# A planner that holds an operation back while the other engine has the SBUF port: linear attention and a Mish feed-forward on one core

## The chip, the cores and the metric

The kernel runs on one core of a Trainium2 chip. A core has five engines, each with its own queue that it works off in order: TensorE (PE, matrix products; its weight loads are PEld), VectorE (DVE), ScalarE (ACT), GpSimd (POOL) and SyncE (SP), which here only issues DMA transfers. Engines wait for one another through semaphores. The metric is the device time of one execution in microseconds, and smaller is better. The kernel before was run three times: 506.88 us in the median, 506.66 to 507.48.

## The reference

The inputs are x (2048 tokens of width 512), weights for attention with 32 heads of 16, and a feed-forward of width 1792; all is float32.

```python
xn = _layernorm(x, axis=-1)
s = _A_ref(xn, A_wqkv, A_w_phi, A_wo)
g = _silu(_B_ref(xn, B_w1, B_b1, B_w2))
return x + s * g

# _A_ref: linear attention
pq = jnp.einsum("bhsd,hdf->bhsf", q, w_phi)      # the same for pk
phi_q = jnp.concatenate([_softmax(pq, axis=-1), _softmax(-pq, axis=-1)], axis=-1)
kv = jnp.einsum("bhsf,bhsd->bhfd", phi_k, v)
z  = jnp.einsum("bhsf->bhf", phi_k)
num = jnp.einsum("bhqf,bhfd->bhqd", phi_q, kv)
den = jnp.einsum("bhqf,bhf->bhq", phi_q, z)[..., None] + 1e-6
o = num / den                                     # then @ wo

# _B_ref: dense, Mish, dense
h = jnp.einsum("bsd,df->bsf", x, w1) + b1
act = h * jnp.tanh(sp)                            # sp = softplus(h)
return jnp.einsum("bsf,fd->bsd", act, w2)
```

## The kernel before

The tokens lie in 16 tiles of 128. Every large product is made in float32r from a high and a low part of each operand (three products in place of one), so each operand is split: ScalarE copies the high part, and VectorE or GpSimd subtracts it to get the low one. The two dense layers use a seven-product scheme on quadrants of their operands (Winograd's form), which needs sums and differences of blocks besides.

The parts, by the letters that the order table uses, each with a number of a tile or block:

- `wq wk wv wo`: a weight is loaded, for q and k multiplied ("folded") with the feature map (tiles `wqf`, `wkf`), and split.
- `N`: load a tile of x, statistics, normalise (`x`), transpose on TensorE (`pt`), split (`xT`), store both forms in DRAM (`scr`, `raw`).
- `K`, `V`, `Q`: the projections of a tile, one product of 12 matmuls each (`k`, `v`, `q`). K and Q are followed by the double softmax: copy (`k0p`), maximum and minimum (`k0m`), two differences (`k0e`), exponential, sum (`k0s`), reciprocal (`k0r`), for K the scaling. `A` adds two key tiles into `kvp` (TensorE) and `zacc`.
- `z`: sums of keys, `zb`. `D`: the denominator of a query tile: `ez` = scores times `zb`, its sum `tz`, `den`, the scaling, and transposes into `ph`. Half of the heads lie in `ph1_0`, the other half in `ph1_1`.
- `Ua`, `Ub`: numerators of eight tiles for one half of the heads (`pn`), split into `oh`, `ol`. `O`: the output projection of a tile (`pw`), kept in DRAM as `so`.
- `L`, `P`, `M`, `R`: blocks of the normalised x, of w1 (first and again), and of w2. `Fa` to `Fd`: the four pieces of a unit of the first dense layer (`fx`, `fy`, `fz`), stored as `hd`.
- `G`: a unit of the second dense layer: load `r`, Mish, sums of blocks on `r` (128 or 256 columns each), split into `ah` and `al` (896 columns), 21 matmuls into `y`. Eight token pairs of seven units make 56, the last five of which are one unit. `E`: the final of a token pair: sums of `y` (`yc`, `yy`), Silu, times the attention output (`sr`), plus x (`xx`), store.

Who does what and when is decided at build time. Every operation is recorded first (class `Program`), each with the engines that may do it: `either` gives VectorE and GpSimd the choice, `copy` and `held` ScalarE and VectorE. The order on TensorE is the order of the parts in the table `ORDER`. For the others, `simulate` plays the program through with assumed costs: at each event it takes, for each engine that is free, the ready operation with the earliest due time (`late`), and `issue` then writes the program out by planned start times. So one instruction queue per engine results, and the chip has no further choice; all of it is issued from one line, L351 before and L360 after.

Two things in `simulate` concern the port. `locks` says which operations need the SBUF port that VectorE and GpSimd share: each of GpSimd's, and VectorE's with two tensor inputs, none of them in PSUM. In `go`, an operation with a lock that starts while the port is held until the time `port` is planned longer by what is left:

```python
if e in o.lock:
    dur += max(0, port - now)
    port = now + dur
```

And `PEN` is added to the due time of an operation on VectorE's list if GpSimd or ScalarE could do it too, so that VectorE takes it later.

Of the kernel before, what the change touches and what calls it, by code (L numbers as in the profile page):

```python
# [38 lines left out]
K7 K6 N12 P0 V6 N10 N11 L0 V8 K11 V9 Fa0 Fa3 K10 A3 A4 V11 V12 V10 Fb3 Fb0 Fc3 Fc0 K12 N14 Fd3 N13 P6 N15 Fd0 K14 A5  # L39
K15 V13 K13 P1 Fa1 Fa6 P4 V15 V14 Q3 Fb6 Fc6 Q2 Fb1 A7 A6 Fc1 Q0 Fd1 P5 z Q7 M2 Fa5 Fd6 D3 Fa4 Q4 Q1 Fb5 Fa2 Fc5 Fb2  # L40
Fb4 Q9 D2 Fc2 D7 Q12 Fd2 Fc4 Fd5 M4 Q5 D4 Q15 L1 Fa9 Fb9 Fd4 Fa11 Fb11 D1 Q6 Fc11 D6 M1 M6 Fc9 Fd11 Fd9 D0 Fa8 D12
Fa13 Fb13 Fc13 M0 Q10 Fb8 Fc8 Fd13 wo1 D9 D15 Fa7 D5 Fb7 Q8 Fd8 M3 Fc7 M5 Q11 Fd7 Fa10 Fa12 D8 D10 Fb12 Fb10 Fc10 Ua0
Fc12 Fd10 Fd12 Ub0 wo0 Q14 Q13 O6 D11 O1 D14 R4 O2 O7 O5 O3 D13 Ua1 O4 Ub1 O0 O11 O15 O12 O8 O13 R0 O9 R5 R1 R6 O14 G0
R2 G1 G2 R3 G3 O10 G4 G5 G6 G7 G8 G9 G10 G11 G12 G13 G14 G15 G16 G17 G18 G19 E0 G20 G21 G22 G23 G24 G25 E1 E2 G26 G27
G28 G29 G30 G31 G32 E3 G33 G34 G35 G36 G37 G38 G39 E4 G40 G41 G42 G43 G44 G45 G46 G47 E5 G48 E6 G49 G50 G51 E7
"""
ACT_SET = {AF.Exp: 1, AF.Silu: 3, AF.Mish: 2}

# [5 lines left out]
class Program:  # L54
# [125 lines left out]
    def simulate(self, at):  # L180
# [17 lines left out]
        pos, now = 0, 0  # L198
# [1 line left out]
        busy = dict(BEGIN)  # L200
        aset = 0
        half = False
        dma = port = 0
        code, fetched, cold = HEAD, 0, 0
        lanes = []
        events = [(t, 2, -1) for t in BEGIN.values()]
# [6 lines left out]
        def fits(o):  # L213
            for t in {self.tag[n] for n in o.new}:
                mine = [n for n in o.new if self.tag[n] == t]
                if t == "ps" and "PE" in o.impl:
                    if free[t] < len(mine):
                        return False
                    continue
                before = 0  # L220
                for n in want[t]:
                    if n in mine:
                        break
                    before += 1
                if free[t] < before + len(mine):
                    return False
            return True
# [59 lines left out]
        while left:  # L287
            if not events:
                bad = [o for o in ops if o.start is None][:5]
                raise RuntimeError(f"no progress at {now}: {[(list(o.impl), o.writes, o.late, o.ready, o.new) for o in bad]} {free}")  # L290
            now, kind, i = heapq.heappop(events)
            todo = [(kind, i)]
            while events and events[0][0] <= now:
                _, kind, i = heapq.heappop(events)
                todo.append((kind, i))
            for kind, i in todo:
                if kind == 0:
                    o = ops[i]
                    o.ready = now
                    if "PE" not in o.impl:  # L300
                        for e in o.impl:
                            heapq.heappush(ready[e], (o.late + (PEN if e == "V" and len(o.impl) > 1 else 0), o.idx))
                elif kind == 1:
                    o = ops[i]
                    left -= 1
                    for n in o.reads | o.writes:
                        if n in uses:
                            uses[n] -= 1
                            if uses[n] == 0:
                                free[self.tag[n]] += 1  # L310
# [674 lines left out]
```

## Time and profile before

| | us |
|---|---|
| median of three runs (lowest, highest) | 506.88 (506.66, 507.48) |
| span of the profiled execution | 505.5 |
| TensorE busy | 496.5 |
| VectorE busy | 434.1 |
| ScalarE busy | 279.4 |
| GpSimd busy | 378.1 |

The span runs from the first to the last instruction. The median of the runs lies 1.4 us above it, for what lies around the span. The granted TensorE clock was 0.999 of full speed, so no throttling has to be told apart here. "Busy" counts an operation from its start to its end, with the time in which it waits for the port; a full engine is therefore not an engine at work all the time. Durations of neighbours on VectorE overlap by some tens of nanoseconds.

### The profile page before, as it was taken

The numbers are of one execution on the slowest core, as the hardware profiler recorded it, in microseconds if no ns is written. First come the engines' busy times: TensorE is split into PE (matmuls) and PEld (weight loads), VectorE is DVE, ScalarE is ACT, GpSimd is POOL, SyncE is SP. The second block draws the span as 40 slices with busy tenths as digits, with TensorE's granted clock in tenths as the row PEclk, the third lists the DMA queues.
The fourth block names the chain that finished last, engine by engine and source line by source line (L and its number), as shares of the span: only waits on it lengthen the run. The fifth ranks groups of instructions, "written<-read, shape, count | busy, mean of one in ns | idle before, by whom it ended". The sixth has DMA issues, their size and how long they took to land.

```text
span 505.5 us, 9803 instructions
## 1 busy us (share of the span) xinstructions
PE 496.5 (98%) x3594; PEld 426.6 (84%) x3594; DVE 434.1 (86%) x651; ACT 279.4 (55%) x412; POOL 378.1 (75%) x271
## 2 busy tenths in 40 slices
PE   8999999999999999999999999899999999999996
PEld 7888888888887888888888777678899999999996
DVE  5999999978879787999997899998768679978764
ACT  4865765465545332553233356587685775958611
POOL 2489999288786565686579558999789779789860
PEclk9999999999999999999999999999999999999999
DMA  8799898829987999889979762825463467665441
GB/s 307 227 336 302 294 346 278 269 105 316 294 295 251 332 319 326 291 233 318 337 240 345 255 229 78 294 89 188 146 209 118 147 204 241 236 199 171 147 146 63
DMA packets 96191, 120.35 MB, mean 238 GB/s; under 512 B 7568, under 2 KB 65040, under 8 KB 96144
## 3 DMA queue, kind: packets, MB, share of 16 engines
q1 hardware_dynamic: 96000, 119.70, 71.2%
q8 instruction: 28, 0.46, 0.4%
q14 instruction: 19, 0.16, 0.1%
q10 hardware_dynamic: 144, 0.03, 0.0%
HBM read 71.08 MB, written 48.63 MB: 237 GB/s over the span
## 4 chain that ended last, share of the span: by engine, by line
PE 89%; DVE 9%; ACT 1%; issue 0%; DMA 0%; DVEq 0%; ACTq 0%
PE y L351 28%; PE fx L351 15%; PE v L351 8%; PE fy L351 8%; PE q L351 8%; PE k L351 7%; PE pw L351 5%; PE fz L351 4%; PE pn L351 2%; PE kvp L351 2%; PE wake L351 1%; PE pt L351 1%; DVE ph L351 1%; DVE tz L351 1%; DVE ol L351 1%; DVE q13e L351 1%
## 5 line engine op out<-in xcount | busy, mean ns | idle before, releaser
L351 POOL TENSOR_TENSOR al<-r,ah 128x896 fp32r<-128x896 f32 (+1 forms) x26 | 55.0, 2123 | 11.2 <-ACT ah L351 9.7
L351 POOL TENSOR_TENSOR r<-r 128x128 f32<-128x128 f32 (+1 forms) x68 | 53.7, 808 | 4.8 <-DVE r L351 2.4
L351 ACT ACTIVATE ah<-r 128x896 fp32r<-128x896 f32 (+1 forms) x56 | 46.2, 853 | 16.5 <-POOL r L351 8.3
L351 DVE TENSOR_TENSOR al<-r,ah 128x896 fp32r<-128x896 f32 (+1 forms) x30 | 40.3, 1358 | 10.7 <-ACT ah L351 5.5
L351 ACT ACTIVATE r<-r 128x512 f32<-128x512 f32 x56 | 33.8, 624 | 19.4 <-DMA r<-hd 19.0
L351 DVE TENSOR_TENSOR r<-r 128x128 f32<-128x128 f32 (+1 forms) x52 | 38.8, 766 | 6.4 <-ACT r L351 3.5
L351 PE MATMUL k<-wkh,xT 128*128 128x512 f32 x128 | 42.2, 393 | 0.0
L351 PE MATMUL q<-wqh,xq 128*128 128x512 f32 x128 | 42.0, 393 | 0.0
L351 PE MATMUL y<-w2t,ah 128*128 128x256 f32 x224 | 40.9, 283 | 0.0
L351 PEld LDWEIGHTS y<-w2t,ah 128*128 128x128 f32 x224 | 34.9, 192 | 0.0
L351 PE MATMUL y<-w2t,al 128*128 128x256 f32 x112 | 31.7, 283 | 0.0
L351 PEld LDWEIGHTS q<-wqh,xq 128*128 128x128 f32 x128 | 24.0, 188 | 5.6 <-issue 0.7
L351 PEld LDWEIGHTS k<-wkh,xT 128*128 128x128 f32 x128 | 24.0, 188 | 5.0
L351 PE MATMUL y<-w2h,ah 128*128 128x256 f32 x96 | 27.2, 283 | 0.0
L351 PE MATMUL y<-w2l,ah 128*128 128x256 f32 x96 | 27.2, 283 | 0.0
L351 PE MATMUL y<-w2h,al 128*128 128x256 f32 x96 | 27.1, 283 | 0.0
L351 PE MATMUL k<-wkl,xT 128*128 128x512 f32 x64 | 24.9, 390 | 0.0
L351 PE MATMUL q<-wql,xq 128*128 128x512 f32 x64 | 24.9, 389 | 0.0
L351 PE MATMUL v<-wv0h,xT 128*128 128x512 f32 x64 | 23.1, 401 | 0.1
L351 PE MATMUL v<-wv1h,xT 128*128 128x512 f32 x64 | 22.3, 390 | 0.0
L351 PEld LDWEIGHTS y<-w2t,al 128*128 128x128 f32 x112 | 21.5, 192 | 0.0
L351 PE MATMUL y<-w2g,al 128*128 128x256 f32 x72 | 20.4, 283 | 0.0
(629 smaller groups left out, 1745.6 us busy)
## 6 DMA issues: line engine op xcount, KB each, us to landing
r<-hd SPq DMA_DIRECT2D x56, 256.0 KB, 3.8
scr<-xT SPq DMA_DIRECT2D x16, 512.0 KB, 5.3
xq<-scr SPq DMA_DIRECT2D x16, 512.0 KB, 5.6
w1b<-w1d SPq DMA_DIRECT2D x14, 512.0 KB, 5.7
w1b<-w1d SPq DMA_DIRECT2D x14, 384.0 KB, 4.7
x<-x SPq DMA_DIRECT2D x16, 256.0 KB, 4.7
raw<-xr SPq DMA_DIRECT2D x16, 256.0 KB, 4.6
fr<-raw SPq DMA_DIRECT2D x8, 512.0 KB, 6.4
```

Of the source, the lines that this page charges most:

```text
L351: getattr(e, m)(*a, **k)
```

## The change

`PEN` goes from 2000 to 0: an operation with a choice is no longer due later on VectorE. The new rule in `simulate`: an operation that locks the port is passed over while another holds it (`port > now + PTOL`, with `PTOL` 0), and the next ready one is tried; the time at which the port comes free is entered as an event, so that what was passed over is looked at again. The table `ORDER` holds the same parts in another order.

```diff
-PEN, HOLD, MARGIN = 2000, 300, 1000
+PEN, HOLD, MARGIN, PTOL = 0, 300, 1000, 0
...
-wq0 wk0 N4 N2 N1 N8 wk1 wv1 wv0 N0 K1 V0 K0 K4 N5 K2 wq1 V2 N3 K5 V3 V1 K3 N9 A0 V4 V5 K8 b1 P2 N7 N6 K9 A1 A2 P3 V7
...
-Fc12 Fd10 Fd12 Ub0 wo0 Q14 Q13 O6 D11 O1 D14 R4 O2 O7 O5 O3 D13 Ua1 O4 Ub1 O0 O11 O15 O12 O8 O13 R0 O9 R5 R1 R6 O14 G0
...
+wk0 wv0 N1 N15 wk1 wq0 K1 N0 K15 N2 K0 N4 wv1 N3 V0 V2 V3 V1 K3 N5 N7 A0 K2 V4 N10 K5 K7 N6 V5 A1 V7 N9 P2 N14 N11 K6
...
+Ua0 Fb10 R0 Fc10 Q13 O3 Q14 D11 Fd10 R1 O1 O4 D14 O7 O2 G7 D13 O5 R3 Ub1 R4 O6 G8 R2 Ua1 G0 O0 O9 O8 G9 G1 O12 O14 O11
...
+G25 G26 G27 G14 G32 G42 E3 G15 G33 G43 G34 G44 G45 G16 G46 G17 G47 G48 E4 G18 G49 E6 G19 G20 G50 E2 G51 E7
...
-                skip = []
+                skip, held = [], False
...
+                    if e in o.lock and port > now + PTOL:
+                        held = True
+                        skip.append((late, i))
+                        if len(skip) > 60:
+                            break
+                        continue
...
+                if held and port > told:
+                    told = port
+                    heapq.heappush(events, (port, 2, -1))
```

In the built program no kind of instruction is new. GpSimd's queue goes from 272 rows to 170, VectorE's from 637 to 744, ScalarE's from 415 to 407; TensorE and SyncE have as many as before.

TensorE at the start, before. `wqf` and `wkf` are folds, `pt` transposes of tiles of x, `k1` the first key product:

```order
L351 MATMUL wqf00_137<-phit_103,wqT00_134 128x128 x4
L351 MATMUL wqf01_138<-phit_103,wqT00_134 128x128 x4
L351 MATMUL wkf00_141<-phit_103,wkT00_130 128x128 x4
L351 MATMUL wkf01_142<-phit_103,wkT01_131 128x128 x4
L351 MATMUL pt4_149<-ident_83,x4_143 128x128 x4
L351 MATMUL pt2_157<-ident_83,x2_151 128x128 x4
L351 MATMUL pt1_165<-ident_83,x1_159 128x128 x4
L351 MATMUL pt8_173<-ident_83,x8_167 128x128 x4
L351 MATMUL wkf10_177<-phit_103,wkT10_132 128x128 x4
L351 MATMUL wkf11_178<-phit_103,wkT11_133 128x128 x4
L351 MATMUL pt0_191<-ident_83,x0_185 128x128 x4
L351 MATMUL k1_194<-wkh0_139,xT1_163 128x512
```

And of the change, the same place:

```order
L360 MATMUL wkf00_136<-phit_103,wkT00_130 128x128 x4
L360 MATMUL wkf01_137<-phit_103,wkT01_131 128x128 x4
L360 MATMUL pt1_147<-ident_83,x1_141 128x128 x4
L360 MATMUL pt15_155<-ident_83,x15_149 128x128 x4
L360 MATMUL wkf10_159<-phit_103,wkT10_132 128x128 x4
L360 MATMUL wkf11_160<-phit_103,wkT11_133 128x128 x4
L360 MATMUL wqf00_164<-phit_103,wqT00_161 128x128 x4
L360 MATMUL wqf01_165<-phit_103,wqT00_161 128x128 x4
L360 MATMUL k1_167<-wkh0_134,xT1_145 128x512
```

The first weight is that of the keys, and two transposes stand ahead of the first key product where five did.

VectorE ahead of the second pair of numerators, before: the last denominators (tiles 13 and 14) and the transposes into `ph1_0` and `ph1_1`, which the products `pn` read:

```order
L351 TENSOR_TENSOR q14r_838<-q14r_838,den14_860 128x64
L351 STREAM_TRANSPOSE ph1_0_724<-q11e_791 128x16x32
L351 TENSOR_TENSOR q13r_845<-q13r_845,den13_877 128x64
L351 STREAM_TRANSPOSE ph1_0_724<-q14e_842 128x16x32
L351 TENSOR_TENSOR q13e_849<-q13e_849,q13r_845 128x1024
L351 STREAM_TRANSPOSE ph1_0_724<-q13e_849 128x16x32
L351 STREAM_TRANSPOSE ph1_1_725<-q11e_791 128x16x32
L351 TENSOR_TENSOR w2e2_934<-w2r2_933 128x256
L351 STREAM_TRANSPOSE ph1_1_725<-q14e_842 128x16x32
L351 STREAM_TRANSPOSE ph1_1_725<-q13e_849 128x16x32
```

And of the change:

```order
L360 TENSOR_TENSOR q14r_849<-q14r_849,den14_868 128x64
L360 TENSOR_TENSOR q13r_840<-q13r_840,den13_880 128x64
L360 TENSOR_TENSOR w2e3_888<-w2r3_887,w2e3_888 128x256
L360 TENSOR_TENSOR q14e_853<-q14e_853,q14r_849 128x1024
L360 TENSOR_TENSOR q13e_844<-q13e_844,q13r_840 128x1024
L360 STREAM_TRANSPOSE ph1_1_619<-q14e_853 128x16x32
L360 STREAM_TRANSPOSE ph1_1_619<-q13e_844 128x16x32
L360 STREAM_TRANSPOSE ph1_0_618<-q14e_853 128x16x32
L360 STREAM_TRANSPOSE ph1_0_618<-q13e_844 128x16x32
L360 TENSOR_TENSOR w2e4_902<-w2r4_901 128x256
```

Both scalings (`q14e`, `q13e`) are on VectorE now, and `ph1_1` is ready first. On TensorE, the table puts `D11 Fd10 O1 O4 O7 O2 G7 O5` between the query product 14 and the numerators `Ub1`, where `O6 O1 O2 O7 O5 O3` stood between product 13 and `Ua1`.

VectorE at the end, before, from the last splits of the second dense layer to the last final (`yc1` and on):

```order
L351 TENSOR_TENSOR al7_5_1176<-r7_5_1174,ah7_5_1175 128x896
L351 TENSOR_TENSOR yc6_1149<-yy6_1150,y60_1129 128x256
L351 TENSOR_TENSOR yy6_1150<-yc6_1149,y61_1130 128x512
L351 TENSOR_TENSOR sr11_1143<-yy5_1141,sr11_1143 128x512
L351 TENSOR_TENSOR yy6_1150<-yy6_1150,y61_1130 128x256
L351 TENSOR_TENSOR xx11_1142<-sr11_1143,xx11_1142 128x512
L351 TENSOR_TENSOR yy6_1150<-yy6_1150,y62_1121 128x512
L351 TENSOR_TENSOR yy6_1150<-yy6_1150,y63_1122 128x512
L351 TENSOR_TENSOR sr13_1152<-yy6_1150,sr13_1152 128x512
L351 TENSOR_TENSOR xx13_1151<-sr13_1152,xx13_1151 128x512
L351 TENSOR_TENSOR yc1_1183<-yc0_1182,y70_1180 128x256
```

And of the change, the last twelve rows of the same stretch; ahead of them stand `al7_2` to `al7_4` and the sums and products of final 6:

```order
L360 TENSOR_TENSOR xx13_1146<-sr13_1147,xx13_1146 128x512
L360 TENSOR_TENSOR xx12_1148<-sr12_1149,xx12_1148 128x512
L360 TENSOR_TENSOR yc2_1159<-yy2_1160,y20_1114 128x256
L360 TENSOR_TENSOR yy2_1160<-yc2_1159,y21_1115 128x512
L360 TENSOR_TENSOR yy2_1160<-yy2_1160,y21_1115 128x256
L360 TENSOR_TENSOR yy2_1160<-yy2_1160,y22_1075 128x512
L360 TENSOR_TENSOR yy2_1160<-yy2_1160,y23_1076 128x512
L360 TENSOR_TENSOR sr5_1162<-yy2_1160,sr5_1162 128x512
L360 TENSOR_TENSOR sr4_1164<-yy2_1160,sr4_1164 128x512
L360 TENSOR_TENSOR xx5_1161<-sr5_1162,xx5_1161 128x512
L360 TENSOR_TENSOR xx4_1163<-sr4_1164,xx4_1163 128x512
L360 TENSOR_TENSOR yc1_1183<-yc0_1182,y70_1180 128x256
```

Before, VectorE did one of the two halves of finals 5 and 6 and GpSimd the other; now it does both halves of 6 and 2, one final behind the other.

More of the change, by code (lines that the diff above doesn't have):

```diff
@@ L37 @@
 ORDER = """
-wq0 wk0 N4 N2 N1 N8 wk1 wv1 wv0 N0 K1 V0 K0 K4 N5 K2 wq1 V2 N3 K5 V3 V1 K3 N9 A0 V4 V5 K8 b1 P2 N7 N6 K9 A1 A2 P3 V7
[L39 to L42, printed above, removed]
-Fc12 Fd10 Fd12 Ub0 wo0 Q14 Q13 O6 D11 O1 D14 R4 O2 O7 O5 O3 D13 Ua1 O4 Ub1 O0 O11 O15 O12 O8 O13 R0 O9 R5 R1 R6 O14 G0
-R2 G1 G2 R3 G3 O10 G4 G5 G6 G7 G8 G9 G10 G11 G12 G13 G14 G15 G16 G17 G18 G19 E0 G20 G21 G22 G23 G24 G25 E1 E2 G26 G27
-G28 G29 G30 G31 G32 E3 G33 G34 G35 G36 G37 G38 G39 E4 G40 G41 G42 G43 G44 G45 G46 G47 E5 G48 E6 G49 G50 G51 E7
+wk0 wv0 N1 N15 wk1 wq0 K1 N0 K15 N2 K0 N4 wv1 N3 V0 V2 V3 V1 K3 N5 N7 A0 K2 V4 N10 K5 K7 N6 V5 A1 V7 N9 P2 N14 N11 K6
+K4 K9 K10 N12 N8 V6 K11 K8 A2 P0 A3 V10 N13 V11 L0 V8 V9 P3 K12 A4 A5 b1 P4 V13 wq1 V14 V15 P6 K14 V12 K13 Fa3 Fa4 Fa0
+Fb0 Fc0 Fb3 Fd0 Fc3 Fb4 Q12 Fc4 Fa6 A7 A6 Fd3 Fb6 P1 Q4 M2 Q3 Fc6 Q7 Q2 P5 Fd6 z Fa5 D3 Fa1 D2 Fa2 Fb2 D7 Fb1 Fb5 Fc5
+Fc1 Fd5 Q1 Fc2 D12 Q6 Fd1 M4 L1 Fd2 Fa9 Fa11 Fd4 Q5 Fb9 Fb11 Fc11 D4 Fc9 Fd11 D1 Q11 M6 D6 M1 Q15 Q9 Q0 Fd9 M0 D0 D5
+Q8 Fa8 Fa13 Fb8 Fc8 Q10 Fb13 M5 Fa7 D9 Fd8 Fb7 Fc7 Fc13 Fd7 D15 D8 M3 D10 Ub0 Fa12 Fd13 Fb12 Fc12 Fa10 Fd12 wo1 wo0
+Ua0 Fb10 R0 Fc10 Q13 O3 Q14 D11 Fd10 R1 O1 O4 D14 O7 O2 G7 D13 O5 R3 Ub1 R4 O6 G8 R2 Ua1 G0 O0 O9 O8 G9 G1 O12 O14 O11
+O13 O10 G10 O15 R6 G11 G2 R5 G12 G13 E1 G35 G36 G3 G4 G5 G6 G37 G28 G38 G21 E0 G29 G22 G39 G40 G41 E5 G23 G30 G31 G24
+G25 G26 G27 G14 G32 G42 E3 G15 G33 G43 G34 G44 G45 G16 G46 G17 G47 G48 E4 G18 G49 E6 G19 G20 G50 E2 G51 E7
 """
@@ L202, in simulate @@
         half = False
-        dma = port = 0
+        dma = port = told = 0
         code, fetched, cold = HEAD, 0, 0
```

## The prediction, on record before the kernel ran

> **What bounds the kernel now.** I read the page's first part, then TensorE's waits, then the chain of waits, then the busy time by stage. The first rows are the span and the engines:
>
> ```profile
> span 505.5 us, 9803 instructions
> PE 496.5 (98%) x3594; PEld 426.6 (84%) x3594; DVE 434.1 (86%) x651; ACT 279.4 (55%) x412; POOL 378.1 (75%) x271
> ```
>
> TensorE is busy for 496.5 of 505.5 us, and the change neither adds nor drops a matmul. What can be won is therefore the 9.0 us in which TensorE stands idle; what can be lost has no such limit. The view of TensorE's own waits names four:
>
> ```profile
> PE pn L351 <- DVE ph L351: 1.4, 1, 1.4
> PE wake L351 <- DVE mhalf L452: 1.1, 1, 1.1
> PE pt L351 <- ACT x L351: 1.0, 1, 1.0
> PE pw L351 <- DVE ol L351: 0.8, 1, 0.8
> ```
>
> The wait before `wake` is the launch and stays. Most of the rest is the drain behind the last product. Three waits of 1.4, 1.0 and 0.8 us are open to a new order, 3.2 us together. Now the stages (columns: window, its length, then busy time of PE, PEld, DVE, ACT, POOL):
>
> ```profile
> 15.00:60.00 45.00, 44.90 (x277) 36.78 (x276) 44.49 (x82) 31.59 (x48) 37.83 (x29) 1.00 0.90 284
> 60.00:125.00 65.00, 65.00 (x596) 53.94 (x596) 59.52 (x86) 36.53 (x53) 50.92 (x33) 1.00 0.81 263
> 286.00:335.00 49.00, 46.82 (x666) 35.85 (x641) 47.30 (x86) 31.58 (x63) 40.38 (x25) 1.00 0.55 186
> 335.00:490.00 155.00, 155.00 (x1060) 144.68 (x1059) 125.50 (x140) 102.95 (x144) 132.72 (x110) 1.00 0.55 177
> ```
>
> VectorE is as full as TensorE between 15 and 60 us (44.49 of 45.00) and nearly so between 286 and 335 (47.30 of 49.00). Where both are full, a microsecond more on VectorE is a microsecond more for TensorE. The chain of waits says the same: it runs through VectorE in both places. Its row of a query product, twelve matmuls in 2.72 us, is the price of a product further down.
>
> ```profile
> 36.02 1.51 DVE k0e L351
> 37.53 0.61 DVE xT L351
> ...
> 141.91 2.72 PE q L351 x12
> ...
> 312.56 1.65 DVE ez L351
> ...
> 318.13 1.55 DVE q13r L351
> ...
> 320.34 1.60 DVE q13e L351
> ```
>
> Some of these pieces are not work. `q13r` is 64 columns wide and holds the chain for 1.55 us. Such time is waiting for GpSimd, as this pair shows:
>
> ```profile
> L351 DVE SCALAR_TENSOR_TENSOR den<-tz x16: 127/188/2332, 178.8 to 316.8; 128x32 f32<-128x32 f32 x16
> 265.78 2.39 POOL L351 TENSOR_TENSOR wo1l<-wor,wo1h 128x1024 fp32r<-128x1024 f32 x1 [0.74 <-DVE ha L351]
> 265.88 2.33 DVE L351 SCALAR_TENSOR_TENSOR den<-tz 128x32 f32<-128x32 f32 x1
> ```
>
> An operation whose median is 188 ns took 2.33 us, because a GpSimd operation of 2.39 us had begun 0.10 us earlier. The change tries to plan such pairs away.
>
> **What moves.** Counted in the built order, 102 tensor-tensor operations go from GpSimd to VectorE: 33 of 128 columns, 24 of 256, 23 of 512, 12 of 896, 10 of 1024. Twelve copies go from ScalarE to VectorE, and ScalarE gets four more table loads. The transfers are the same 354 rows on the SyncE queue in another order. Prices:
>
> ```profile
> L351 DVE TENSOR_TENSOR al<-r,ah 128x896 fp32r<-128x896 f32 x20 | 28.3, 1428 | 6.9 <-ACT ah L351 4.7 <-POOL al L351 2.0
> 470.10 1.08 DVE L351 TENSOR_TENSOR al<-r,ah 128x896 fp32r<-128x896 f32 x1
> L351 POOL TENSOR_TENSOR al<-r,ah 128x896 fp32r<-128x896 f32 x20 | 46.8, 2350 | 11.2 <-ACT ah L351 9.7 <-DVE al L351 1.3
> L351 DVE TENSOR_TENSOR r<-r 128x128 f32<-128x128 f32 x36 | 26.4, 746 | 1.1 <-POOL r L351 1.0
> L351 POOL TENSOR_TENSOR r<-r 128x128 f32<-128x128 f32 x44 | 30.0, 697 | 3.5 <-DVE r L351 2.4 <-PE y L351 0.6
> L351 POOL TENSOR_TENSOR r<-r 128x256 f32<-128x256 f32 x24 | 24.2, 1012 | 1.3 <-ACT r L351 1.3
> L351 DVE TENSOR_TENSOR xx<-sr,xx 128x512 f32<-128x512 f32 x6 | 9.3, 1558 | 1.3 <-POOL sr L351 1.2
> L351 POOL TENSOR_TENSOR xx<-sr,xx 128x512 f32<-128x512 f32 x8 | 12.4, 1555 | 2.3 <-DMA xx<-x 2.2
> L351 DVE TENSOR_TENSOR xT<-pt,xT 128x512 fp32r<-128x512 f32 x16 | 10.6, 675 | 1.7 <-ACT xT L351 1.7
> L351 DVE TENSOR_TENSOR u<-u,sr 128x256 f32<-128x256 f32 x4 | 1.7, 425 | 1.0 <-ACT u L351 1.0
> 245.49 1.22 DVE L351 TENSOR_TENSOR q0e<-q0e,q0r 128x1024 f32<-128x1024 f32 x1
> L351 DVE TENSOR_REDUCE tz<-ez 128x64 f32<-128x1024 f32 x16 | 19.0, 1199 | 0.0
> ```
>
> Undisturbed, VectorE takes 0.425 us for 256 columns, 0.675 for 512, 1.08 for 896, 1.22 for 1024, and by an estimate from the first two 0.30 for 128. The moved work is 33 x 0.30 + 24 x 0.425 + 23 x 0.675 + 12 x 1.08 + 10 x 1.22 + 12 x 0.675 = 69 us on VectorE. GpSimd loses, at its means, 33 x 0.70 + 24 x 1.01 + 23 x 1.56 + 12 x 2.35 + 10 x 2.4 = 135 us and falls to about 243.
>
> If every port wait stayed, VectorE would be busy for 434 + 69 = 503 us, longer than TensorE: then VectorE bounds the kernel. But waits are in the 434: 20 x (1.428 - 1.08) = 7.0 in `al`, 36 x (0.746 - 0.30) = 16.1 in the short `r`, and 6 x (1.558 - 0.675) = 5.3 in `xx`, so 28 in three groups alone. Without those VectorE is at 475. I take 480: the waits shrink at least with GpSimd's work, and a plan that holds operations back removes more, though not all. That is 46 us more than before, and the question is where.
>
> Mostly it is late. The units of the second dense layer (335 to 490) run almost wholly on VectorE now; there it was busy for 125.5 of 155 us and GpSimd for 132.7. About 80 of the 102 operations are of this stage (33 of 128 columns, 18 of 256, 16 of 512, 12 of 896), 9.9 + 7.7 + 10.8 + 13.0 = 41 us, which would make 166 with the old waits and about 138 without the 28. That fits under TensorE's 155, and I price it at 0, from 0 to +10.
>
> **Start: -0.8 us.** TensorE ran three folds and five transposes before the first `k`:
>
> ```profile
> 12.38 1.36 PE L351 MATMUL pt<-ident,x 128*128 128x128 f32 x8 [1.01 <-ACT x L351]
> 15.98 0.48 PE L351 MATMUL k<-wkh,xT 128*128 128x512 f32 x1
> 5.59 0.69 DVE L351 BATCH_NORM_STATS2 st<-x 128x6 f32<-128x512 f32 x1 [1.11 <-DMA x<-x]
> 6.56 1.95 PE L351 MATMUL wqf<-phit,wqT 128*128 128x128 f32 x16
> 7.23 1.07 POOL L351 TENSOR_TENSOR rs<-rs,mhalf 128x1 f32<-128x1 f32 x2 [5.30 <-DVE rs L351]
> 9.14 1.53 ACT L351 ACTIVATE x<-x,nb,rs 128x512 f32<-128x512 f32 x2 [0.88 <-DVE nb L351]
> ```
>
> Now there are three folds and two transposes. Before, 800 KB (scores' table, `wqT`, first `x`) were there at 5.59 us. In the new order the same 800 KB are both `x` tiles, the table and the first half of `wkT`, so the first fold can start when the warm-up ends, at 6.56, and takes 1.8 us (1.95 less the overlap), to 8.4. The second tile needs statistics (ends about 6.3), two small sums (0.3), both powers on GpSimd (1.07), a bias on VectorE behind the first tile's normalising (0.7) and one normalising on ScalarE (1.53 / 2): 9.2. Its transpose follows, then two folds of 1.8: `k` starts at about 13.4 where it started at 15.98. Three transposes are still owed, 1.36 / 2 = 0.6 each as the row has it. Gain 15.98 - 13.4 - 1.8 = 0.8. Bounds: -1.4 (the transposes hide their overhead) and +0.6 (`phit` now stands behind the first statistics).
>
> **Middle: -2.2 us.** Before, six attention products (2.72 us each, 16.3) stood between the last query product and the second pair of numerators, and VectorE's row of work in that time needed 1.4 more. Now two dense products, four attention products, a unit of the second layer and one more attention product stand there: 7 x 2.72 = 19.0 us. VectorE's rows from that query's score copy to the transposes that the numerator reads add up to 17.1 us by the prices above and the reductions' 1.2. So the 1.4 should go, if port waits there stay under 1.9. The 0.8 of `pw <- ol` goes as well: its attention product now comes 6.8 us behind the numerator instead of 5.4. Bounds: -2.2 and +2 (GpSimd has two products with `zb` in that chain).
>
> **Keys and values: +0.9 us.** All sixteen tiles' keys and values now come before the first dense product, where eleven keys and ten values came before. An estimate from the rows: TensorE needs 32 x 2.72 = 87 us for them, and with transposes, folds and key sums some 106; VectorE needs about 5.8 us a tile (statistics 0.69, split 0.675, maximum, minimum and differences at 0.675 each, the sum at 1.2, small ones), and with the weights' splits, the scaling and `zacc` some 107. VectorE has no slack of its own there, only what TensorE's lag behind it leaves. Some unplanned waits will show: from 0 to 5, and I take 0.9, nearer the old stage, for which the waits view names none.
>
> End: the drain behind the last product does not change, 0. Sum: -0.8 - 2.2 + 0.9 + 0 = -2.1. The profiled span 505.5 becomes 503.4; the median of the runs, 506.88, lies 1.4 above that span, so the forecast is 504.8 us.
>
> [...]
>
> **The rivals.** First: the waits only change place. VectorE has 46 us more to do, and each gain of 3.0 us is paid back in stalls of under a microsecond. For it: the full windows above. Against it: the two middle gaps are covered by more TensorE work now. Time 506.5, chance 0.18.
>
> Second, slower: VectorE bounds the key and value stage. Its place is the run of sixteen keys; its price two waits for a whole GpSimd operation (2.39 in the row), less a little that TensorE's queue hides, 4.5 in place of the 0.9. It decides once the stalls there pass the 3.0 us gained elsewhere. For it: 44.49 of 45.00. Time 506.9 - 3.0 + 4.5 = 508.4, chance 0.16.
>
> Third, slower: the end. All four multiplies and adds of a final are on VectorE, and two finals (tiles 6 and 2) stand between the last units' splits and the last final, where GpSimd took half of each:
>
> ```profile
> 489.75 1.62 POOL L351 TENSOR_TENSOR xx<-sr,xx 128x512 f32<-128x512 f32 x1
> 492.44 0.42 DVE L351 TENSOR_TENSOR yc<-yc,y 128x256 f32<-128x256 f32 x1 [2.22 <-ACT yc L351]
> 495.62 1.21 DVE L351 TENSOR_TENSOR yc<-yc,y 128x256 f32<-128x256 f32 x3 [2.76 <-PE y L351]
> ```
>
> A final is two operations of 256 and seven of 512 columns, 5.6 us, some 7 with its wait for Silu. Between the last two rows lie 26 matmuls, 0.12 us each; tile 2's last unit is done 24 + 52 = 76 matmuls, 9.1 us, ahead of the product that the last final needs. From 2 us of lag on, the end moves. With 6 us of lag: 504.8 + 4 = 508.8, chance 0.10.
>
> Fourth: everything opens, 1.4 at the start, 2.2 in the middle and nothing new: 506.9 - 3.6 = 503.3, chance 0.12.
>
> **How the numbers follow.** The forecast has 0.44, with a range of its own from 503.8 to 506.0. This kernel tells a change from none at about 0.2%, 1.0 us: faster is under 505.9, slower over 507.9. Faster is 0.42 of the forecast and the fourth, 0.54; the same is 0.02 of the forecast and 0.17 of the first, with 0.01 from the slower cases, 0.20; slower is the second and third with the rest, 0.26. The range from 503.0 to 508.7 leaves out a little of the fourth and the worse half of the slower ones.
>
> **What would show it.** Right: the `pn <- ph` and `pw <- ol` waits gone from TensorE's waits; `k` begins at about 13.4 us; VectorE busy near 480 and GpSimd near 245 us; `al` on VectorE near 1.1 us; no TensorE wait on a VectorE tile over 0.5 us before 125 us. Wrong: TensorE waiting for `xT`, `k..e` or a bank in the keys; GpSimd's fall without a fall of VectorE's means; the last `yc` waiting for VectorE and not for TensorE.

## The result and the profile after

The changed kernel takes 509.74 us in the median of four runs (508.2 to 510.4), the kernel before 506.77 us beside it (506.08 to 507.48). The ratio is 1.0052 with a 95% interval from 1.0033 to 1.007: slower by half a per cent, where 2.1 us less were forecast. A second set of six runs gave 509.06 against 507.18 us, ratio 1.0039 (1.0024 to 1.0055).

The page of the changed kernel, first part (span, then busy time, share and instructions of each engine):

```profile
span 506.5 us, 9767 instructions
PE 496.2 (98%) x3594; PEld 425.4 (84%) x3594; DVE 430.1 (85%) x765; ACT 278.8 (55%) x404; POOL 244.1 (48%) x169
```

TensorE's own waits there (us in total, times, longest):

```profile
PE pn L360 <- DVE ph L360: 2.7, 1, 2.7
PE wake L360 <- DVE mhalf L461: 1.1, 1, 1.1
PE fx L360 <- ACT hc L360: 0.7, 1, 0.7
PE fx L360 <- ACT hb L360: 0.4, 1, 0.4
PE wkf L360 <- DVE rs L360: 0.3, 1, 0.3
PE fx L360 <- DVE ha L360: 0.3, 1, 0.3
```

GpSimd lost a third of its work and VectorE, which took it over, is busy for 4 us less than before: most of its waiting for the port is gone. Yet the wait for `ph`, 1.4 us before, is 2.7 us now, and the dense products `fx` have three waits that the kernel before did not have. Of the old ones only `pw <- ol` and `pt <- x` are gone.

Where the time went is read from the busy time by stage. Two rows of the kernel before that the prediction does not show (window, length, then busy time of PE, PEld, DVE, ACT, POOL):

```profile
0.00:60.00 60.00, 57.72 (x362) 48.96 (x362) 53.50 (x109) 39.33 (x60) 41.64 (x43) 1.00 0.89 292
125.00:286.00 161.00, 161.00 (x841) 132.39 (x855) 141.78 (x219) 66.93 (x91) 111.04 (x64) 1.00 0.88 299
```

and the same view of the changed kernel:

```profile
0.00:60.00 60.00, 58.52 (x430) 49.96 (x431) 53.62 (x121) 41.41 (x64) 42.17 (x42) 1.00 0.92 299
60.00:125.00 65.00, 64.95 (x537) 53.57 (x536) 62.05 (x88) 34.35 (x48) 45.93 (x32) 1.00 0.81 263
125.00:286.00 161.00, 159.57 (x931) 129.60 (x930) 144.26 (x229) 66.18 (x92) 81.42 (x49) 1.00 0.84 287
286.00:335.00 49.00, 46.27 (x450) 36.66 (x464) 45.52 (x81) 30.58 (x52) 36.50 (x21) 1.00 0.58 195
335.00:490.00 155.00, 155.00 (x1171) 143.93 (x1140) 116.86 (x233) 104.23 (x145) 38.08 (x30) 1.00 0.57 184
```

TensorE's idle time, length less busy time, went from 2.28 to 1.48 us in the first 60 us, from 0 to 0.05 in the keys, from 0 to 1.43 between 125 and 286, from 2.18 to 2.73 between 286 and 335, and stayed at 0 in the second dense layer. That is -0.80 + 0.05 + 1.43 + 0.55 = +1.2 us; the profiled spans differ by 1.0. So the start brought what it should, and the loss lies in one stretch, from the query products to the last pair of numerators.

The medians differ by more than the profiled spans, because the executions of the changed kernel fall into two groups: of its second six, three spanned 506.2 to 506.7 us at a granted clock of 1.000, and three 508.0 to 508.5 at 0.996 to 0.997, while the kernel before lay between 504.2 and 506.0 at 0.998 to 1.000 throughout. The profile shown is one of the shorter kind, whose times (507.9 to 508.4 us) lie only some 1 us above the kernel before; the longer kind makes the rest of the difference, and is explained below by the last experiments' rows.

Now the stretch itself. The timeline of the changed kernel at 212 us (start, duration, operation), first VectorE's:

```profile
212.52 1.22 DVE L360 TENSOR_TENSOR t11l<-t,t11h 128x1024 fp32r<-128x1024 f32 x1
213.65 3.43 DVE L360 TENSOR_TENSOR t31l<-t,t31h 128x1024 fp32r<-128x1024 f32 x1
217.01 1.21 DVE L360 TENSOR_TENSOR t41l<-t,t41h 128x1024 fp32r<-128x1024 f32 x1
```

and GpSimd's:

```profile
212.74 3.26 POOL L360 TENSOR_TENSOR ez<-q4e,zb 128x1024 f32<-128x1024 f32 x1 [1.88 <-DVE t L360]
```

Three equal operations take 1.22, 3.43 and 1.21 us. The GpSimd product `ez` came in 0.2 us after the first had begun, waited for its end and then held the port; the second waited for it. The planner had meant it otherwise. These are the times with which it laid out the program (a model inside the kernel, not a measurement) beside the real ones:

```
operation                  planned start   real start (us)
t11l   VectorE                 211.67         212.52
t31l   VectorE                 212.80         213.65
t41l   VectorE                 213.94         217.01
ez (tile 4)   GpSimd           215.21         212.74
```

In the plan GpSimd is passed over until `t41l` ends. In the program nothing says so: the order within GpSimd's queue is kept, but `ez` waits only for what it reads and writes, and the row names the end of VectorE's `t` (212.6 us) as what released it. It starts 2.5 us ahead of its plan, and the wait that the rule planned away comes back, on the other engine. The planner of the kernel before lets an operation start at once and adds the wait for the port to its duration, as with `den` and `wo1l` in the prediction's rows. Up to 330 us VectorE lies at most 2.9 us behind that plan, and up to 7.9 us behind the new one.

The same view at 307 us, where 19 us later the late numerators begin, VectorE:

```profile
307.72 2.38 DVE L360 SCALAR_TENSOR_TENSOR den<-tz 128x32 f32<-128x32 f32 x1
```

and GpSimd:

```profile
307.64 2.41 POOL L360 TENSOR_TENSOR ez<-q13e,zb 128x1024 f32<-128x1024 f32 x1
```

Summed over the trace (each VectorE operation's duration above the fastest tenth of its operation and shape, where that is over 0.15 us), the waits fell from 29.2 to 18.0 us ahead of 327 us and from 54.8 to 2.6 behind. The big saving lies where TensorE was the bound in any case; ahead of 327 us, 11 us were saved against some 17 us of work that VectorE took over (the moved operations at undisturbed prices).

In both meetings the operation that came second took longer by about what the first still had to do: `ez` behind `t11l` by 0.87 us (3.26 in place of the 2.39 it takes alone, below), where `t11l` had 1.00 left, and `t31l` behind `ez` by 2.21 (3.43 against 1.22), where `ez` had 2.35 left. Not every operation of VectorE takes part. Of those of the changed kernel that began while a GpSimd operation had more than 0.6 us left, the 21 reductions of 1024 columns took 1.21 us in the median and the 45 operations on two tensors of 512 columns with one in PSUM 0.68, both as with GpSimd idle; the four on two tensors of 1024 columns in SBUF took 1.71 to 3.43 in place of 1.22. The same happened in the keys (2.2 us at 94 us, where TensorE lost 0.05 us in the whole stage), but what it cost came in the query stage.

### The profile page after: what moved, and what is told of

Same layout as the page of the kernel before. It is cut to its first block, busy times and chain, and to the rows that moved or that the text cites. A ratio compares the mean times of both kernels' runs of the same rounds, so it can differ in the third digit from the quotient of the medians.

```text
span 506.5 us, 9767 instructions
## 1 busy us (share of the span) xinstructions
PE 496.2 (98%) x3594; PEld 425.4 (84%) x3594; DVE 430.1 (85%) x765; ACT 278.8 (55%) x404; POOL 244.1 (48%) x169
## 4 chain that ended last, share of the span: by engine, by line
PE 42%; DVE 12%; issue 1%; DMA 1%; ACT 1%; POOL 0%; ACTq 0%; DVEq 0%
PE y L360 27%; PE pw L360 6%; PE fx L360 3%; PE pn L360 2%; DVE tz L360 2%; DVE ph L360 2%; PE fy L360 1%; PE q L360 1%; DMA w1b<-w1d 1%; DVE den L360 1%; PE fz L360 1%; DVE u L360 0%; DVE q6r L360 0%; DVE hc L360 0%; DVE ha L360 0%
## 5 line engine op out<-in xcount | busy, mean ns | idle before, releaser
L360 DVE TENSOR_TENSOR al<-r,ah 128x896 fp32r<-128x896 f32 (+1 forms) x43 | 42.6, 1011 | 9.5 <-ACT ah L360 8.0
L360 POOL TENSOR_TENSOR al<-r,ah 128x896 fp32r<-128x896 f32 (+1 forms) x13 | 24.9, 1927 | 47.4 <-ACT ah L360 32.9
L360 POOL TENSOR_TENSOR r<-r 128x128 f32<-128x128 f32 (+1 forms) x17 | 13.6, 812 | 49.4 <-DVE r L360 26.9
L360 DVE TENSOR_TENSOR r<-r 128x128 f32<-128x128 f32 (+1 forms) x103 | 30.6, 340 | 7.6 <-ACT r L360 6.9
L360 ACT ACT_TABLE_LOAD x15 | 19.2, 1283 | 7.8 <-DVE yy L360 6.4
```

Of the source, the lines that this page charges most:

```text
L360: getattr(e, m)(*a, **k)
```

## Which half of the change it is

The first four runs undo one half of the change each: the planner (`PEN` 2000 and the rule off), the order, and the planner in one stage alone.

```diff
e1, on the changed kernel
-PEN, HOLD, MARGIN, PTOL = 0, 300, 1000, 0
+PEN, HOLD, MARGIN, PTOL = 2000, 300, 1000, 10**9
e2, on the changed kernel
-ORDER = (the new table)
+ORDER = (the table of the kernel before)
```

> The new order of TensorE's parts with the old planner (penalty 2000 ns, rule off). Theory 1, VectorE bounds the query stage: in the changed kernel its own work up to the last transposes is 278 us at undisturbed prices against 260 before, while the waits that the rule saves there came to 12.5 us only. Here that work is 255 us, so VectorE is there earlier than in either kernel, TensorE's wait for ph (2.7 us in the changed kernel, 1.4 before) and its waits in the first dense layer (1.4 together) go, and the time is 504.5 to 505.5 us. Theory 2, the new order itself is at fault, because it puts the parts that wait too close together: TensorE's waits for hc, hb and ph stay, and the time is 509 to 510 us, as for the whole change.

> The old order of TensorE's parts with the new planner (penalty 0, rule on). VectorE's own work up to the last transposes is 267.5 us, 8 more than before. Theory 1 (VectorE's sum of work and port waits decides): plus 8 of work, minus some 12 of port waits, so VectorE is a little earlier than before, the wait for ph shrinks below 1.4 us and the time is 505 to 507 us. Theory 2 (the order is at fault): about 506.8 us, as before. Theory 3 (the planner's choice is bad with any order): 509 us or more, with new waits of TensorE for VectorE before 330 us.

```diff
e3, on the changed kernel (e4 has < in place of >=)
-(PEN if e == "V" and len(o.impl) > 1 else 0)
+((PEN if now >= 330000 else 2000) if e == "V" and len(o.impl) > 1 else 0)
-if e in o.lock and port > now + PTOL:
+if e in o.lock and port > now + PTOL and now >= 330000:
```

> The changed kernel, but penalty 0 and the rule hold only from the planner's 330 us on (second dense layer and end); up to there the old planner. Theory 1 (the loss is VectorE's extra work in the query stage): VectorE's own work up to the last transposes is 259 us as before, port waits there near 30 us again, and the time is 504.5 to 506 us. Theory 2 (order at fault): 509 to 510. Theory 4 (the loss is in the second dense layer or the end, where nearly all splits and finals are on VectorE): 509 to 510 as well, with VectorE's wait ahead of the last yc replaced by TensorE's work ending later; told from theory 2 by the first run.

> The changed kernel, but penalty 0 and the rule hold only up to the planner's 330 us; from there the old planner, with the second dense layer shared between VectorE and GpSimd as before. Theory 1: nothing changes up to the last transposes (278 us of work there), the waits for ph, hc and hb stay, and the time is 509 to 510 us as for the whole change; what the rule gained in the second dense layer was hidden under TensorE anyway. Theory 4 (loss in the second layer or the end): 506 to 507 us.

The first, the third and the fourth lie far from everything that was expected; the second fits theory 3 alone (509 us or more, with a new wait ahead of 330 us). Measured against 507.04 us of the kernel before: the order alone 558.41 us (ratio 1.1008, 1.0985 to 1.103), the planner alone 516.5 (1.0187, 1.0173 to 1.0201), the new planner only late 543.56 (1.0726, 1.0707 to 1.0746), only early 526.91 (1.0402, 1.038 to 1.0424). TensorE's longest waits with the order alone:

```profile
PE y L360 <- DVE yc L360: 8.5, 2, 7.7
PE fz L360 <- DVE hb L360: 6.4, 1, 6.4
PE kvp L360 <- POOL k8e L360: 4.4, 1, 4.4
```

with the planner alone:

```profile
PE pn L360 <- DVE ph L360: 5.3, 1, 5.3
```

and with the new planner early only:

```profile
PE y L360 <- DVE yc L360: 8.7, 2, 7.8
PE y L360 <- DVE yy L360: 3.5, 3, 2.5
```

A table of parts is good only with the planner that it was laid out for: each half alone costs 9 to 51 us, both together 2 to 3. So these runs cannot say which half of the pair costs the 3 us, and theories 1 and 2 are not decided by them. Theory 3, that the planner's choice is bad with any order, is left by the second run and falls with the next section, where the new planner with the new order beats the kernel before. The runs do say something of the second dense layer: with the old planner from 330 us on, TensorE waits there for `yc` and `yy`, 12 us together, and the kernel is 17 us slower than with the new one throughout (526.91 against 509.7). The relief there is needed by this table; it is not a gain over the kernel before.

The planner's own end of the last product foretold most of this, but not the change:

```
kernel                     planned end of products   measured span (us)   difference
before                            500.7                   505.5              4.8
order alone (e1)                  559.6                   556.4             -3.2
planner alone (e2)                510.1                   514.5              4.4
new planner late (e3)             531.6                   541.3              9.7
new planner early (e4)            515.6                   525.2              9.6
changed kernel                    493.8                   506.5             12.7
```

Behind the last product come some 4.8 us of drain. The last product of the kernel before ends where its plan says. The changed kernel was planned 6.9 us shorter and lies 8 us behind its plan: it is not that nothing was to be won, but that the chip did not follow. Part by part, TensorE's lag behind the plan grows from 1.3 us at 128 us to 2.2 at 222, 4.0 at 276, 7.1 at 326 and 7.9 at the end. This set the next theory.

## Making the hold real

Theory 5: the loss is the hold that stands only in the plan. The test keeps plan and order as they are and makes GpSimd wait in the program. Ahead of a GpSimd operation that the rule had passed over stands a GpSimd subtraction on one column, which reads a result of the VectorE operation that held the port (by `locks` that can also be a copy or a one-tensor operation outside PSUM).

```diff
+                        if e == "G":
+                            o.hold = owner
...
+            y = o.hold
+            if o.eng == "G" and y is not None and y.eng == "V":
+                t = (first column of y's result)
+                nc.gpsimd.tensor_tensor(self.pin, t, t, op=ALU.subtract)
             for m, a, k in o.impl[o.eng][1]:
```

> The changed kernel with the same plan and the same order on every engine; only ahead of each of the 45 GpSimd operations that the new rule passed over in the plan stands a GpSimd operation on one column that reads the result of the VectorE operation behind which the planner held it. So GpSimd really starts behind it. Theory 5 (the hold exists only in the plan: nothing in the program makes GpSimd wait, it starts as soon as its inputs are there, gets ahead of the VectorE operation and makes that one wait instead): VectorE's waits up to 327 us fall from about 15 us to under 5, TensorE's waits for ph, hc and hb go, and the time is 499 to 503 us. Theory 1 (VectorE's moved work is too much whatever GpSimd does): 508 to 511 us, as the changed kernel.

The second does it at four places only, `(o.part, y.part) in (("A4", "L0"), ("D4", "L1"), ("D5", "D6"), ("D13", "D11"))`:

> As the run before, but only at four places: zacc of key pair 4 behind t2 of the first load, the product of tile 4 with zb behind t4l, that of tile 5 behind the normalising of tile 6, that of tile 13 behind den of tile 11. There VectorE's t3, t3l, q6r and den11 waited 2.2, 2.2, 1.7 and 2.2 us, 8.3 together. Theory 5: most of the 8.3 us on VectorE go, the wait for ph goes, 503 to 506 us. Theory 1: 508 to 511 us.

The control has the same 45 operations, reading the constant `mhalf`:

> Control for the two runs before: the same 45 one-column operations on GpSimd, but they read a constant and wait for nothing. Theory 5 and theory 1 both: as the changed kernel, 508 to 511 us, since 45 short operations delay GpSimd by some 0.1 to 0.2 us each and it has half its time free. If it is under 506 us, the gain of the runs before was the delay alone and not the order.

> The changed kernel once more, for its spread and for a profile of one of its longer executions. All theories: median 508.5 to 510.5 us. Theory 5 asks that a longer execution differ from the shorter one by further VectorE operations of 0.1 to 0.7 us that wait for a whole GpSimd operation, with TensorE's wait for ph longer by as much; theory 6 (the granted clock alone makes the spread) asks for the same waits and longer matmuls.

All on one chip, beside 507.18 us of the kernel before: all 45 holds 504.64 us (ratio 0.9957, 0.9943 to 0.997), four holds 504.55 us (0.9951, 0.9938 to 0.9965), the control 508.63 (1.0028, 1.0017 to 1.0039), the changed kernel 509.06. Four small operations are worth 4.5 us, and they beat the kernel before by 0.5%; the same operations without the wait are worth 0.4 us, which is within the spread of both. Theory 5 stands, theory 1 in its strict form (VectorE's moved work is too much whatever GpSimd does) falls.

The control is not without any effect on the order: its profile (span 507.1 us) has `t31l` at 3.42 us and the `fx` waits of the changed kernel, but `den` at 0.30 us, because the added operations happened to delay `ez` past it, and so 1.1 us of waiting for `ph`. TensorE idles where it does not in the changed kernel (0.8 us between 60 and 125 us, 0.4 in the second dense layer); their cause was not looked for.

The size for 45 holds was missed: 499 to 503 us were expected, and VectorE's waits ahead of 327 us, by the sum above, fell to 9.9 us, not under 5 (four holds: 11.9; control 17.2). The 41 further holds clear the wait for `ph` wholly, but TensorE idles 0.8 us in the second dense layer instead; they bring nothing more that these runs can tell. The four holds lie in their range (503 to 506).

The kernel with four holds, VectorE's timeline at the first place shown above:

```profile
212.74 1.22 DVE L375 TENSOR_TENSOR t11l<-t,t11h 128x1024 fp32r<-128x1024 f32 x1
213.88 1.22 DVE L375 TENSOR_TENSOR t31l<-t,t31h 128x1024 fp32r<-128x1024 f32 x1
215.02 1.22 DVE L375 TENSOR_TENSOR t41l<-t,t41h 128x1024 fp32r<-128x1024 f32 x1
```

GpSimd's timeline there, the added operation `pin` first:

```profile
216.31 0.19 POOL L370 TENSOR_TENSOR pin<-t41l 128x1 f32<-128x1 f32 x1 [5.22 <-DVE t41l L375]
216.46 2.39 POOL L375 TENSOR_TENSOR ez<-q4e,zb 128x1024 f32<-128x1024 f32 x1
```

VectorE's timeline at the second place:

```profile
305.60 0.18 DVE L375 SCALAR_TENSOR_TENSOR den<-tz 128x32 f32<-128x32 f32 x1
```

TensorE's waits of over half a microsecond, of the same kernel:

```profile
PE wake L375 <- DVE mhalf L477: 1.1, 1, 1.1
PE pn L375 <- DVE ph L375: 0.9, 1, 0.9
```

and its busy time by stage:

```profile
125.00:286.00 161.00, 161.00 (x941) 131.72 (x940) 143.19 (x234) 67.45 (x94) 82.12 (x51) 1.00 0.85 290
286.00:335.00 49.00, 48.11 (x559) 37.71 (x559) 43.65 (x80) 32.44 (x54) 37.12 (x22) 1.00 0.60 202
```

`t31l` is back at 1.22 us, `den` at 0.18, `ez` itself at 2.39 in place of 3.26. GpSimd stood still for 5.2 us for this, and all that waited for it was VectorE, 0.27 us ahead of the sum of `ez` at 218.9 us. TensorE's idle time is 0 instead of 1.43 us between 125 and 286, and 0.9 instead of 2.7 between 286 and 335. The plan's 6.9 us are not all there: the span, 502.8, is 2.7 under that of the kernel before.

## Which of the four places counts

The next three runs have one or two of the four holds each; the fourth has no holds and relieves VectorE of work instead: it leaves out the scaling of the query tiles 3, 6 and 11.

```diff
e9    (o.part, y.part) in (("A4", "L0"),)
e10   (o.part, y.part) in (("D4", "L1"), ("D5", "D6"))
e11   (o.part, y.part) in (("D13", "D11"),)
e12, on the changed kernel
+            if o.eng == "V" and len(o.impl) > 1 and o.part in ("D3", "D6", "D11") and any(n.startswith("q" + o.part[1:] + "e") for n in o.writes):
+                continue
```

> Of the four holds only the first: zacc of key pair 4 really starts behind t2 of the first load, so that VectorE's t3 (2.2 us of waiting at 94 us) is free. VectorE's lateness against the plan came down again after that place (from 2.8 us at 117 to 0.1 at 179 us), because the plan leaves it gaps there. Theory 5: the gain is lost in those gaps, 508 to 510 us, as the changed kernel. If every microsecond of waiting on VectorE counted: 506.5 to 508 us.

> Only the second and third hold: the product of tile 4 with zb behind t4l, and that of tile 5 behind the normalising of tile 6; 3.9 us of waiting on VectorE at 214 and 236 us. From 210 us on the plan has no gap on VectorE, its lateness went from 0.9 to 5.6 us there and stayed above 3. Theory 5: TensorE's waits for hc and hb (1.4 us) go, and the wait for ph shrinks by what is left: 505 to 507 us. If only the last place counts: 508.5 to 510 us.

> Only the fourth hold: the product of tile 13 with zb behind den of tile 11; 2.2 us of waiting on VectorE at 308 us, 15 us ahead of the pair of numerators that waited for ph. Theory 5: the wait for ph falls from 2.7 us to about 0.5, the waits for hc and hb at 221, 256 and 265 us stay: 506 to 507.5 us, and the granted clock stays at 1.00 behind the place.

> The changed kernel without any hold, but VectorE leaves out the normalising of the query tiles 3, 6 and 11 (three operations of 1024 columns at 181, 238 and 319 us, 1.22 us each; those tiles go into the numerators without their scale). The matmuls are the same. Theory 5 in its wider form (TensorE waits because VectorE is late, whether by waiting or by work): 2.4 us less ahead of ph in the packed stretch, so the wait for ph is nearly gone, the waits for hc and hb before 238 us stay: 506 to 507.5 us. If GpSimd or ScalarE set the end and VectorE's waits only show it: 508.5 to 510 us.

Beside 506.95 us of the kernel before: the early hold 510.6 us (ratio 1.0061, 1.0046 to 1.0076), the two in the middle 506.92 (0.9994, 0.9978 to 1.0009), the late one 506.97 (0.9997, 0.9988 to 1.0006), VectorE relieved 506.15 (0.9982, 0.9973 to 0.9991). The last three lie in their ranges; the first is 0.6 us over its own (five of its six executions are of the longer kind). The executions with the middle holds spread widest of all, 504.57 to 509.6 us; why was not followed up.

Against the 509.06 us of the changed kernel (measured on another chip, where the kernel before took 507.18) the middle and the late holds are worth 2.1 us each, and together with the early one 4.5. Some 1 us of each is the longer kind of execution, which is rare with the middle holds and absent with the late one; against the shorter kind they are worth 1.2 us each. The early one alone is worth nothing, though the wait it removes (2.2 us) is as long as the others: with it or without it, VectorE lies 2.7 us behind its plan at 117 us, since gaps in its work take such a delay up. Behind 210 us its delay rose from 0.9 to 5.6 us and was still 3.2 at 276.

Leaving out 3.7 us of VectorE's work brings 2.9 us without touching GpSimd: TensorE waits because VectorE is late in this stretch, whether by waiting or by work. The wait for `ph` is not nearly gone there, as was expected, but 1.6 us:

```profile
PE pn L362 <- DVE ph L362: 1.6, 1, 1.6
```

TensorE's waits with the middle holds:

```profile
PE pn L375 <- DVE ph L375: 2.7, 1, 2.7
PE y L375 <- DVE yc L375: 0.9, 1, 0.9
PE fx L375 <- ACT ha L375: 0.2, 1, 0.2
```

and with the late one:

```profile
PE pn L375 <- DVE ph L375: 0.9, 1, 0.9
PE fx L375 <- ACT hc L375: 0.7, 1, 0.7
PE fx L375 <- ACT hb L375: 0.5, 1, 0.5
```

The middle holds clear all but 0.2 us of the `fx` waits, and TensorE, 1.7 us earlier then, waits for `ph` as long as ever; I had expected that wait to shrink. The reason is in VectorE's timeline of the changed kernel, at the copy of query product 14, with which the work for `ph` begins:

```profile
304.68 0.69 DVE L360 COPY q14p<-q 128x512 f32<-128x512 f32 x1 [0.28 <-PE q L360]
```

VectorE waits for TensorE here. Whatever delay it has brought along, both engines start even, and only what happens behind this row can make the wait for `ph`: from here to the end of the second transpose into `ph1_1` VectorE takes 21.7 us, 4.8 of them port waits, and TensorE's seven products 19.2. The late hold, which lies behind the row, clears two thirds of the `ph` wait and leaves the `fx` waits; the scaling of tile 11, left out at 319 us in the last run, lies behind it as well.

The profile with the early hold caught one of the longer executions. From 125 us on its program is that of the changed kernel. TensorE's timeline there, from the wait for `ph` on (in brackets the wait):

```profile
326.87 4.08 PE L375 MATMUL pn<-ph,kvw 32*32 32x256 f32 x128 [2.73 <-DVE ph L375]
```

in the changed kernel's profile:

```profile
326.41 2.76 PE L360 MATMUL pn<-ph,kvw 32*32 32x256 f32 x128 [2.73 <-DVE ph L360]
```

The wait is 2.73 us in both. In one execution the clock stays at full speed, in the other it is halved for some 3.4 us, and the same 128 products take 1.3 us longer. What differs is where the wait lies on the clock's own time. The times at which the clock changes lie whole multiples of 3.41 us apart: 3.98 and 505.74 us in the changed kernel's profile (147 of them), 6.27 and 504.62 in that of the kernel before (146), 326.66 and 330.07 with the early hold (one). Whether it falls can be read from the stretch of 3.41 us that ends there. TensorE's busy time with the early hold in these stretches (behind the bracket with the matmuls: granted clock, DMA share, GB/s):

```profile
323.24:326.66 3.42, 0.89 (x4) 1.00 0.01 2
326.66:330.07 3.41, 3.21 (x100) 0.50 0.21 82
330.07:333.48 3.41, 3.41 (x56) 1.00 0.00 0
```

in the changed kernel's first profile:

```profile
321.42:324.84 3.42, 2.26 (x10) 1.00 0.01 2
324.84:328.25 3.41, 1.84 (x101) 1.00 0.22 82
```

in its second (a wait of 2.72 us):

```profile
322.24:325.66 3.42, 1.58 (x7) 1.00 0.01 2
```

and, with the order alone, at a wait of 1.91 us:

```profile
200.91:204.32 3.41, 1.50 (x7) 1.00 0.74 211
204.32:207.74 3.42, 3.42 (x9) 0.50 0.92 359
```

With the early hold 2.53 us of the wait fall into one stretch, and the clock is halved for the next. In the changed kernel the stretches split the wait, 1.16 and 1.57 us, and it stays. In these rows it fell behind stretches with 2.53 and 1.91 us of idle time and stayed up behind those with 1.84, 1.57 and 1.16; in the profiles of the two kernels no stretch between the rise of the clock and the last product has more than 1.57. Where the stretches lie differs from execution to execution: the clock first came up at 6.27 us in the profile of the kernel before and at 3.98 in that of the changed kernel.

The spans of these two profiles are 508.0 and 506.5 us, and the executions of the changed kernel fall into the same two groups. One halved stretch of 3.4 us in 508 makes a mean clock of 0.997, which most of the longer executions have (0.996 to 0.997). That they have it at this very place is argued from that; no profile of one of them was taken. The run with the new planner early only, the same program up to 330 us, shows it as well (2.78 us of waiting, then 4.08 us for the products).

## Why the prediction was wrong, point by point

**Start, -0.8 us: right.** TensorE's idle time in the first 60 us fell by 0.80; the wait of 1.0 us for `x` is gone, and one of 0.3 us ahead of `wkf` has come. `k` begins at 12.45 us instead of 15.98 (13.4 was forecast). That it came earlier than forecast is luck of the execution: the warm-up products (`wake`) took 4.52 us in this profile and 5.61 in that of the kernel before, and in the other profiles with this start `k` begins at 12.4 to 13.2 us.

**Keys and values, +0.9 us: too dear.** TensorE lost 0.05 us there. The second rival, VectorE bounding this stage, fell with it: VectorE does wait (2.2 us at 94 us), but the early hold shows that nothing hangs on it.

**Second dense layer, 0: right, and for the reason given,** 155.00 of 155.00 us busy. VectorE's total, though, is 430 us and not 480: I let the waits shrink as GpSimd's work, and behind 327 us they went almost altogether. The splits `al` of 896 columns on VectorE have 1.12 us in the mean, and GpSimd is at 244 us, as forecast.

**Middle, -2.2 us: this is the step that failed.** TensorE lost 0.55 us between 286 and 335 us instead of gaining 2.2. The 0.8 of `pw <- ol` did go; the wait for `ph` grew from 1.4 to 2.7. The step set 17.1 us of VectorE's work against 19.0 us on TensorE, and both sizes were right: 21.7 less 4.8 of port waits, and 19.2. Its condition, port waits under 1.9 us, was the term without a reason, and it was 4.8: 2.2 in `den`, 1.1 in one `tz`, and the rest in three others. Its bound of +2 named the cause, GpSimd's two products with `zb`; the longest wait is `den` behind one of them, and the late hold, which orders just these two, took 1.8 us off the wait for `ph`. What I had not asked is whether the plan's holds exist in the program. The row quoted for the port, `den` at 2.33 us beside `wo1l`, was of the kernel before; the new `den` row at 2.38 us beside `ez` is its twin.

**Query products, no term at all: +1.43 us.** Between 125 and 286 us the sum had nothing. `t31l`, `den`, a `tz` and `q6r` waited between 213 and 238 us and brought VectorE from 0.9 to 5.6 us behind its plan; the `fx` waits came at 222, 257 and 266 us, behind the first or all of these, and the middle holds cleared all but 0.2 us of them. With the two misses (+2.75 and +1.43) and the keys (-0.85), the -2.1 us of the sum become the +1.2 us of idle time that the stages show.

**The clock, not in the sum.** A wait of 2.7 us sometimes halves the clock behind it: 0 or about 1.5 us on the span, which takes the median beyond every rival. The planner's model in both kernels assumes such a term (`IDLE` and `COLD`: behind more than 2.1 us of idle time TensorE's work costs double for 3.4 us); the sum had none, because it expected the wait to go. The first rival, waits that only change place, was the nearest in kind, and its price (506.5 us) was short by the port waits in these two places and by the clock. The third, the end, fell: TensorE is busy up to the last products and the last `yc` waits for TensorE as before.

The signs named beforehand would have told it: the `ph` wait stayed, so the middle was wrong; `k`, `al` and GpSimd came near what was written, VectorE's 480 us did not.

## What to carry to other kernels

A planner's "not now" is worth only what the program enforces: where an operation is to stay behind another of a different engine, give it something to wait for, one column was enough here (`pin`, 0.19 us), or model the engine as it is and let it start at once. Before crediting saved waits, ask where they are saved: ahead of a consumer that is late, or under an engine that is the bound anyway; and count the work that moves in the same stretch. Where a queue has no gaps, small delays add up until the next gap (here from 0.9 to 5.6 us behind 210 us); where it has some, the same delay costs nothing (here the 2.2 us at 94 us), so it is the last gap ahead of the consumer from which to count, and the port waits behind that gap are the ones to price.

## What was not expected of the hardware

TensorE's clock fell behind stalls much shorter than one of its stretches of 3.41 us: 1.91 us of idle time in one were enough (the order alone, 200.9 to 204.3 us), while 2.73 us that two stretches shared were not (the changed kernel). It came back at the end of a halved stretch in which TensorE had idled for 0.20 us (the early hold, 326.66 to 330.07 us); behind one with at least 1.38 us it stayed halved (the new planner early only, 473.5 to 477.0 us).

GpSimd pays for a collision too, though less: `ez` took 3.26 us where it came second and 2.39 where it was alone.

The time around the span, within one execution, differs: 507.32 - 505.2 = 2.1 us for the kernel before, 508.12 - 506.4 = 1.7 for the changed kernel and 504.48 - 502.8 = 1.7 with four holds. No run was made to find the cause of those 0.4 us, so it stays open. The 1.4 us ahead of the prediction set the median of three executions beside the span of one.
